# Feed-forward operands stored in four spaced quarters and read four columns at a time, last columns first

## The chip, the cores and the metric

The kernel runs on one core of one Trainium2 chip. The metric is device time in microseconds; the median of three runs of the kernel before is 530.65 us (530.53 to 530.72). The core works with five engines: TensorE (PE, matrix products; its weight loads are listed apart as PEld), VectorE (DVE), ScalarE (ACT), GpSimd (POOL) and SyncE (SP, which issues nearly all DMAs). Operands lie in the on-chip memory SBUF, in 128 partitions; TensorE writes its results to PSUM.

## The reference, cut to what matters

A gated recurrence over 768 steps, for 4 batches and 8 heads of width 48, gives a matrix x of 3072 tokens by 384 channels; a gated feed-forward layer follows.

```python
for t in range(S):                                  # S = 768, D = 48
    state = alpha[:, :, t, :, None] * state + k_t (x) v_t
    y[:, :, t] = q_t @ state
x = y.transpose(0, 2, 1, 3).reshape(3072, 384)
gate = 1 / (1 + exp(-(x @ w_gate)))                 # 384 x 1536
val = x @ w_val                                     # 384 x 1536
out = (gate * val) @ w_out                          # 1536 x 384
```

## The kernel before, in words

Tokens are taken in `NG` = 6 groups of `T` = 512. In each group the recurrence is worked out in chunks, by 4 units (pairs of heads); units 0 to 5 (function `unit`) use chunks of 128 tokens, units 6 to 23 (function `late`) chunks of 64. A unit ends in `finish`: ACT copies its output y from PSUM as a rounded high part (line 500, or line 489 in group 0), DVE subtracts that from y and stores the rest as a low part (lines 501 and 491), and, from group 1 on, SP moves both from the tile `yt` to the right partitions of `x` by DMA (line 508).

The feed-forward layer runs in 72 steps (function `step`), 12 blocks of 128 hidden channels in each of the 6 groups. All weights and the moving operands are split in such a high and a low part of type fp32r, and a product is taken as high by high, high by low and low by high (`PAIRS`). So a step has 9 matmuls for the gate and 9 for the value (line 297, three parts by three tiles of 128 input channels) and 9 for the output (line 741, three parts by three tiles of 128 output channels), 27 in all. Each loads its own 128x128 weights and streams 512 columns, one token each, of 4 bytes. Between them ACT takes the sigmoid (line 728), DVE multiplies (line 730), ACT rounds the product to `hh` (line 732) and DVE stores the rest in `hl` (line 733).

What is moved is read in order of its address: `xin(g)[:, i, b, :]` and `h[a][:, 0:T]` are 512 consecutive words of a partition. Tiles stand in SBUF one behind the other. The tile `between`, 40 words of which one is used, stands between `sg` and `hh`. By the sizes of the tiles, `x0`, `x1`, `hh`, `hl` and all weight tiles of the program before start at the same address modulo 512 bytes.

The order of the work on each engine is set when the program is built: `Plan` simulates the engines with estimated times, the table `MOVES` shifts single pieces, and the result is issued as it stands. Before the first product 60 places for bf16 matmuls on the identity matrix (line 705, `warm`) are planned, which nothing reads; those that come ahead of the first feed-forward product are issued.

Of the kernel before, what the change touches and what calls it, by code (L numbers as in the profile page):

```python
# [8 lines left out]
F32 = mybir.dt.float32  # L9
F32R = mybir.dt.float32r  # L10
# [6 lines left out]
ALU = mybir.AluOpType  # L17

P = 128
B, H, S, D = 4, 8, 768, 48  # L20
DM, DF = 384, 1536
# [16 lines left out]
    tuple(((2 * p + j) * D, p - 1, R * j, D) for p in range(1, NP) for j in range(2))  # L38
EARLY = 6
TURNED = 4  # L40


WIDTH = EH + 3 * T + 1
# [216 lines left out]
def vec(n):  # L260
    return 0.07 + n / 960


def act(n):
    return 0.13 + n / 1200
# [35 lines left out]
def chunked(ctx, tc, rows, vc, vh, weights_in, out, const, ident, flags, weights, within):  # L301
# [8 lines left out]
    def slot(tag, size):  # L310
        slots[tag] = [const.tile([P, size], F32, name=f"first_{tag}", tag=tag), 0]
        held[tag] = []

    for f in range(6, NF):
        slot(f"w{f}", 2 * WF)
    slot("x1", NK * 2 * T)

    def borrow(tag, *shape):
        t, at = slots[tag]
# [33 lines left out]
    tops = [(f"top{i}", sb.tile([P, WF // 2], U32, name=f"top{i}")) for i in range(3)]  # L353
    r_top = Ring(tops)
    r_kn = ring("kn", 1, CH, P, early=[borrow("w6", CH, P) for _ in range(2)])
    r_yt = ring("yt", 1, 2, T, dtype=F32R)
    r_A = ring("A", 2, 2, T, early=[borrow("x1", 2, T) for _ in range(2)])
    (pickn, pick), (sparen, spare) = borrow("w7", NK, P), borrow("w7", 2, T)
    pick, spare = pick.bitcast(F32R), spare.bitcast(F32R)
# [7 lines left out]
    tiny = sb.tile([P, EH], F32, name="tiny")  # L367
    starts = sb.tile([P, NG * NP, EH], F32, name="starts")
    sts = [sb.tile([P, EH + 1, D], F32, name=f"st{p}") for p in range(NP)]
    r_x = [const.tile([P, NK, 2, T], F32R, name="x0", tag="x0")]  # L370
    r_sg = ring("sg", 1, T)
    between = sb.tile([P, 40], F32, name="between")
    r_hh, r_hl = ring("hh", 2, T, dtype=F32R), ring("hl", 2, T, dtype=F32R)
    r_at = ring("at", 3, 512, pool=ps)
    r_pg, r_pv, r_po = ring("pg", 1, 512, pool=ps), ring("pv", 1, 512, pool=ps), ring("po", NM, 512, pool=ps)
    r_bank = Ring([*r_at.tiles, *r_po.tiles, *r_pg.tiles])
# [5 lines left out]
    nc.vector.memset(d1g[C][:, 0:T:C], 1.0)  # L382
    nc.vector.memset(d1f, 0.0)
    nc.vector.memset(tiny, 1e-30)
    nc.gpsimd.memset(mask[C], 1.0)
    nc.gpsimd.affine_select(out=mask[C], in_=mask[C], pattern=[[1, C]], compare_op=ALU.is_ge, fill=0.0, base=0, channel_multiplier=-1)

# [55 lines left out]

    def xin(g):
        if g % 2 == len(r_x):
            r_x.append(const.tile([P, NK, 2, T], F32R, name="x1", tag="x1"))
        return r_x[g % 2]

    def decays(u, size, t, inn, tin):
# [34 lines left out]
    def finish(g, p, t, pyn, py):  # L484

        x_n = f"x{g % 2}"
        if g == 0 and p:
            x, hi, lo = xin(0)[:, p - 1], (x_n, p - 1, "hi"), (x_n, p - 1, "lo")
            plan.add("scalar", act(T), t["y"], lambda: nc.scalar.copy(out=x[:, 0], in_=py[:, 0:T]), [pyn], [hi])
            plan.add("vector", vec(T), t["y"], lambda: nc.vector.tensor_tensor(  # L490
                out=x[:, 1], in0=py[:, 0:T], in1=x[:, 0], op=ALU.subtract), [pyn, hi], [lo])
            xparts.setdefault(0, []).extend([hi, lo])
            return
        if g == 0:
            plan.add("scalar", act(T), t["y"], lambda: nc.scalar.copy(out=spare[:, 0], in_=py[:, 0:T]), [pyn], [(sparen, "s")])
            plan.add("vector", vec(T), t["y"], lambda: nc.vector.tensor_tensor(
                out=spare[:, 1], in0=py[:, 0:T], in1=spare[:, 0], op=ALU.subtract), [pyn, (sparen, "s")], [(sparen, "k")])
            return
        ytn, yt = r_yt.next()
        plan.add("scalar", act(T), t["y"], lambda: nc.scalar.copy(out=yt[:, 0], in_=py[:, 0:T]), [pyn], [(ytn, 0)])  # L500
        plan.add("vector", vec(T), t["y"], lambda: nc.vector.tensor_tensor(
            out=yt[:, 1], in0=py[:, 0:T], in1=yt[:, 0], op=ALU.subtract), [pyn, (ytn, 0)], [(ytn, 1)])
        for ch, k, row, m in PLACES:
            j, src = divmod(ch, D)
            if j // 2 != p:
                continue
            src += R * (j % 2)
            plan.add("sync", (ISSUE, 0.3 + 0.6 * m * T * 8 / RATE), t["y"], lambda row=row, m=m, k=k, src=src: nc.sync.dma_start(
                out=xin(g)[row:row + m, k].bitcast(F32), in_=yt[src:src + m].bitcast(F32)), [(ytn, 0), (ytn, 1)],
                [(x_n, k, ch), *(before("x1") if g == 1 else [])])  # L510
            xparts.setdefault(g, []).append((x_n, k, ch))
# [200 lines left out]
    def step(s):  # L712
        g, f = divmod(s, NF)
        got = {}
        for nm, r, dt in (("g", r_pg, 0.0), ("v", r_pv, 0.33)):
            pn, pt = (r_three if g else r).next()
            got[nm] = (pn, pt)
            def ahead(nm=nm, pt=pt, tiles=None):
                if nm == "v":
                    opened.append(s)  # L720
                products(nc, pt[:, 0:T], lambda a, i: weights.part(nm, a, f)[:, i], lambda b, i: xin(g)[:, i, b, :], tiles)

            for tiles in ([range(NK - 1), range(NK - 1, NK)] if s < 2 else [range(NK)]):
                plan.add("tensor", (MM * 3 * len(tiles), 1.0), s + dt, lambda ahead=ahead, tiles=tiles: ahead(tiles=tiles),
                    [*weight(nm, f), *(x for x in xparts[g] if x[1] in tiles)], [pn])
        soon = s > NF + 2
        (sgn, sg), (hhn, hh), (hln, hl) = r_sg.next(), r_hh.next(), r_hl.next()
        plan.add("scalar", act(T), None, lambda: nc.scalar.activation(out=sg, in_=got["g"][1][:, 0:T], func=AF.Sigmoid), [got["g"][0]], [sgn], soon=soon)  # L728
        pvn, pv = got["v"][0], got["v"][1][:, 0:T]
        plan.add("vector", vec(T), None, lambda: nc.vector.tensor_tensor(out=pv, in0=pv, in1=sg, op=ALU.mult), [sgn], [pvn], soon=soon)  # L730
        last = s == NG * NF - 1
        plan.add("scalar", act(T), None, lambda: nc.scalar.copy(out=hh, in_=pv), [pvn], [hhn], soon=soon)  # L732
        plan.add("vector", vec(T), None, lambda: nc.vector.tensor_tensor(out=hl, in0=pv, in1=hh, op=ALU.subtract), [pvn, hhn], [hln], soon=soon)
        h = (hh, hl)
        if f == 0:
            pso[:] = [r_po.next() for _ in range(NM)]

        def back(m, some):
            for i in some:
                a, b = PAIRS[i]  # L740
                nc.tensor.matmul(out=pso_now[m][1][:, 0:T], lhsT=weights.part("o", b, f)[:, m * P:(m + 1) * P], rhs=h[a][:, 0:T],  # L741
                                 start=(f == 0 and i == 0), stop=(f == NF - 1 and i == 2))

        pso_now = list(pso)
        for some, hs in (((0, 1), [hhn]), ((2,), [hln])):
            for m in range(NM):
                plan.add("tensor", (MM * len(some), 1.0), s + 1 + 0.66 + (0.1 * m + 0.01 * some[0] - 0.5 if last else 0.01 * m + 0.1 * some[0]), lambda m=m, some=some: back(m, some),
                         [*hs, *weight("o", f)], [pso_now[m][0]])
        if f == NF - 1:
            for m in range(NM):  # L750
                (pn, pt), (on, to) = pso[m], ob[m]
                over = [(on, "u"), (on, "l")] if g == 0 else []
                halves = 2 if (m == NM - 1 if last else g in (3, 4)) else 1
                n = T // halves
                for half in range(halves):
                    cs, queue = slice(half * n, (half + 1) * n), "scalar" if last and m % 2 == 0 and half == halves - 1 else "sync"
                    if m % 2:
                        plan.add("vector", vec(n), s + 1.9, lambda pt=pt, to=to, cs=cs: nc.vector.tensor_copy(out=to[:, cs], in_=pt[:, cs]), [pn], [("ob", m, half), *over])
                    else:
                        plan.add("scalar", act(n), s + 1.9, lambda pt=pt, to=to, cs=cs: nc.scalar.copy(out=to[:, cs], in_=pt[:, cs]), [pn], [("ob", m, half), *over])  # L760
                    plan.add(queue, (ISSUE, n / T), s + 1.9, lambda to=to, m=m, cs=cs, queue=queue: getattr(nc, queue).dma_start(
                        out=out[m * P:(m + 1) * P, g * T + cs.start:g * T + cs.stop], in_=to[:, cs]), [("ob", m, half)])
# [60 lines left out]
def general(tc, rows, decay, values, out, weights):  # L823
# [3 lines left out]
    with ExitStack() as ctx:  # L827
# [32 lines left out]
        with tc.For_i(0, NG, 1) as g:  # L860
# [7 lines left out]
            for f in range(NF):  # L868
                pg, pv = (ps.tile([P, T], F32, name=f"gp{nm}") for nm in "gv")
                for nm, pt in (("g", pg), ("v", pv)):  # L870
                    products(nc, pt, lambda a, i: weights.part(nm, a, f)[:, i], lambda c, i: x[:, c, i])
                sg, hf, h = sb.tile([P, T], F32, name="gsg"), sb.tile([P, T], F32, name="ghf"), sb.tile([P, 2, T], F32R, name="gh")
                nc.scalar.activation(out=sg, in_=pg, func=AF.Sigmoid)
                nc.vector.tensor_tensor(out=hf, in0=pv, in1=sg, op=ALU.mult)
# [1 line left out]
                nc.vector.tensor_tensor(out=h[:, 1], in0=hf, in1=h[:, 0], op=ALU.subtract)  # L876
                for m in range(NM):
                    for n, (a, c) in enumerate(PAIRS):
                        nc.tensor.matmul(out=po[m], lhsT=weights.part("o", c, f)[:, m * P:(m + 1) * P], rhs=h[:, a],
                                         start=(f == 0 and n == 0), stop=(f == NF - 1 and n == 2))  # L880
            o = sb.tile([P, NM, T], F32, name="go")
            for m in range(NM):
# [58 lines left out]
```

## Time and profile before

| | |
|---|---|
| median of 3 runs | 530.65 us |
| profiled execution, first to last instruction (its span) | 528.8 us |
| between the span and the median of the runs | 1.85 us |
| PE busy | 519.7 us, 98% of the span |
| DVE busy | 398.7 us, 75% |
| ACT busy | 163.4 us, 31% |
| POOL busy | 88.5 us, 17% |
| granted TensorE clock | 0.999 of full speed |

The profile is of one execution. A matmul's duration there runs from its start to the modelled end of its results, and consecutive matmuls overlap; so what a chain of matmuls costs is read from the distance of their starts, not from the sum of durations. A group of n merged instructions in a timeline lasts n - 1 distances and one duration. DVE's share is uneven: over 95% from 30 to 90 us, 15% to 30% after 440 us, when the recurrence is done.

### The profile page before, as it was taken

To read this page: it belongs to the slowest core of one execution; us is meant where nothing else is said; L and a number is where in the kernel's file an instruction comes from. 1 tells how busy PE (TensorE), PEld (TensorE's weight loads), DVE (VectorE), ACT (ScalarE), POOL (GpSimd) and SP (SyncE) were. 2 spreads that over 40 slices of the span, in tenths; PEclk is the share of its full clock that TensorE was granted. 3 is DMA by queue.
4 is the path that set the end of the run, shared out by engine and by line. 5 is a ranking of instruction groups with operands and counts; after the bars stand their busy time and mean duration, and the time that the engine had idled before them with its cause. 6 is when DMAs were issued, how large, how long until landed. Compare 5 with 4: busy or idle time off the path is not lost.

```text
span 528.8 us, 10387 instructions
## 1 busy us (share of the span) xinstructions
PE 519.7 (98%) x4114; PEld 422.4 (80%) x4114; DVE 398.7 (75%) x866; ACT 163.4 (31%) x304; POOL 88.5 (17%) x127
## 2 busy tenths in 40 slices
PE   7999999999999999999999999999999999999996
PEld 3777888888888887888888888887888888888884
DVE  8999999888989999969888969889878532222221
ACT  2566666624112222222222321222322212311211
POOL 4532131103121122111121301211401100000000
PEclk9999999999999999999999999999999999999999
DMA  8757696830623333331423412403412011100001
GB/s 317 293 163 241 218 279 189 222 93 20 179 78 91 105 106 116 81 91 31 121 73 88 131 42 90 113 11 120 151 30 67 2 30 31 60 1 0 2 0 64
DMA packets 23093, 54.70 MB, mean 103 GB/s; under 512 B 3712, under 2 KB 10880, under 8 KB 23040
## 3 DMA queue, kind: packets, MB, share of 16 engines
q1 hardware_dynamic: 22752, 53.60, 33.8%
q8 instruction: 34, 0.56, 0.4%
q10 hardware_dynamic: 288, 0.39, 0.2%
q14 instruction: 19, 0.16, 0.1%
HBM read 41.39 MB, written 4.72 MB: 87 GB/s over the span
## 4 chain that ended last, share of the span: by engine, by line
PE 94%; DVE 4%; issue 0%; POOL 0%; ACT 0%; DVEq 0%
PE po L741 29%; PE pv L297 20%; PE pg L297 20%; PE at L297 16%; PE at L648 2%; PE pg L691 1%; PE at L655 1%; PE pv L691 1%; PE at L691 1%; DVE F L460 1%; DVE G L456 1%; PE at L476 1%; PE at L539 0%; PE pg L591 0%; PE pg L597 0%; DVE st L568 0%
## 5 line engine op out<-in xcount | busy, mean ns | idle before, releaser
L741 PE MATMUL po<-hh,w 128*128 128x512 f32 x432 | 116.1, 395 | 0.0
L297 PE MATMUL pv<-x,w 128*128 128x512 f32 x468 | 115.2, 390 | 0.0
L297 PE MATMUL pg<-x,w 128*128 128x512 f32 x459 | 112.9, 390 | 0.0
L297 PEld LDWEIGHTS pv<-x,w 128*128 128x128 f32 x468 | 87.6, 188 | 18.4
L297 PEld LDWEIGHTS pg<-x,w 128*128 128x128 f32 x459 | 85.9, 188 | 18.0 <-ACT w L428 0.2
L741 PEld LDWEIGHTS po<-hh,w 128*128 128x128 f32 x432 | 79.6, 188 | 17.0
L297 PE MATMUL at<-x,w 128*128 128x512 f32 x369 | 90.7, 390 | 0.1
L297 PEld LDWEIGHTS at<-x,w 128*128 128x128 f32 x369 | 69.1, 188 | 14.9 <-issue 0.5
L639 DVE STREAM_TRANSPOSE kn<-in 32x128 f32<-32x128 f32 x224 | 67.8, 303 | 5.0 <-PE at L655 1.2
L741 PE MATMUL po<-hl,w 128*128 128x512 f32 x216 | 64.4, 391 | 0.0
L679 POOL TENSOR_TENSOR vs<-st,dec 64x384 f32<-64x384 f32 x36 | 30.6, 850 | 162.3 <-DVE st L674 161.1
L464 POOL TENSOR_TENSOR in<-in,G 128x512 f32<-128x512 f32 x21 | 28.2, 1342 | 145.0 <-DVE G L456 46.9
L741 PEld LDWEIGHTS po<-hl,w 128*128 128x128 f32 x216 | 40.5, 188 | 8.7
L674 DVE SCALAR_TENSOR_TENSOR st<-st,dec,at 128x48 f32<-128x48 f32 x144 | 38.1, 264 | 7.7 <-PE at L655 1.9
L730 DVE TENSOR_TENSOR pv<-pv,sg 128x512 f32<-128x512 f32 x31 | 21.3, 687 | 29.7 <-PE pv L297 29.6
L730 DVE TENSOR_TENSOR at<-at,sg 128x512 f32<-128x512 f32 x21 | 14.4, 687 | 31.3 <-PE at L297 31.1
L732 ACT CAST hh<-pv 128x512 fp32r<-128x512 f32 x31 | 18.2, 586 | 55.1 <-DVE pv L730 55.1
L728 ACT ACTIVATE sg<-pg 128x512 f32<-128x512 f32 x31 | 18.5, 598 | 53.7 <-PE pg L297 53.7
L730 DVE TENSOR_TENSOR pg<-pg,sg 128x512 f32<-128x512 f32 x20 | 13.7, 687 | 27.1 <-PE pg L297 27.1
L661 DVE TENSOR_TENSOR A<-at,mask 64x256 f32<-64x256 f32 x72 | 30.4, 422 | 1.3
L728 ACT ACTIVATE sg<-pv 128x512 f32<-128x512 f32 x21 | 12.6, 598 | 50.1 <-PE pv L297 50.1
L460 DVE TENSOR_TENSOR_SCAN F<-in,d1f 128x512 f32<-128x512 f32 x22 | 27.6, 1257 | 0.3
(162 smaller groups left out, 508.1 us busy)
## 6 DMA issues: line engine op xcount, KB each, us to landing
in<-in_rows_dram SPq DMA_DIRECT2D x18, 516.5 KB, 3.9
raw<-in_w_dram SPq DMA_DIRECT2D x12, 575.8 KB, 4.7
x<-yt SPq DMA_DIRECT2D x30, 192.0 KB, 3.4
first_w<-in_w_dram SPq DMA_DIRECT2D x10, 575.8 KB, 4.9
A<-in_rows_dram SPq DMA_DIRECT2D x36, 128.0 KB, 3.9
v<-in_vc_dram SPq DMA_DIRECT2D x22, 192.0 KB, 5.0
vs<-in_vh_dram SPq DMA_DIRECT2D x36, 96.0 KB, 3.5
out_dram<-raw SPq DMA_DIRECT2D x10, 256.0 KB, 2.2
```

Source lines behind the costliest of these rows:

```text
L297: nc.tensor.matmul(out=dst, lhsT=lhs(a, i), rhs=rhs(b, i), start=(n == 0 and i == 0), stop=(n == len(todo) - 1 and i == NK - 1))
L460: plan.add("vector", scan(n), after(t["G"], 0.01), lambda: nc.vector.tensor_tensor_scan(out=F, data0=az[:, 0:n], data1=d1f, initial=0.0, o ...
L464: plan.add(e, vec(n) if e == "vector" else pool_(n), t["kt"], lambda: getattr(nc, e).tensor_tensor(out=kT, in0=kT, in1=G, op=ALU.mult), [g ...
L639: nc.vector.transpose(out=kn[32 * b:32 * b + 32, :, 32 * a:32 * a + 32], in_=blocks[32 * a:32 * a + 32, b])
L661: plan.add("vector", 0.42, t["mask"], lambda pa=pa, j=j, i=i: nc.vector.tensor_tensor(out=A[other[j], j].rearrange("p (c i t) -> p i c t", ...
L674: nc.vector.scalar_tensor_tensor(out=st[:, c + 1, :], in0=st[:, c, :], scalar=dec[:, c:c + 1], in1=pas[c % 2][1][:, T // 2 + c // 2 * D:T ...
L679: plan.add("gpsimd", pool_(EH * D), t["sd"], lambda j=j: nc.gpsimd.tensor_tensor(out=vs[own[j], j], in0=st[own[j], 0:EH], in1=dec[own[j]]. ...
L691: nc.tensor.matmul(out=py[R * j:R * j + D, cs], lhsT=vs[r, j, c, :], rhs=A[r, j, cs], start=True, stop=True)
L728: plan.add("scalar", act(T), None, lambda: nc.scalar.activation(out=sg, in_=got["g"][1][:, 0:T], func=AF.Sigmoid), [got["g"][0]], [sgn], s ...
L730: plan.add("vector", vec(T), None, lambda: nc.vector.tensor_tensor(out=pv, in0=pv, in1=sg, op=ALU.mult), [sgn], [pvn], soon=soon)
L732: plan.add("scalar", act(T), None, lambda: nc.scalar.copy(out=hh, in_=pv), [pvn], [hhn], soon=soon)
L741: nc.tensor.matmul(out=pso_now[m][1][:, 0:T], lhsT=weights.part("o", b, f)[:, m * P:(m + 1) * P], rhs=h[a][:, 0:T], start=(f == 0 and i == ...
```

## The change

Each tile of moving operands (`x0`, `x1`, `hh`, `hl`, and `yt`, from which x is filled) becomes 576 words long instead of 512 for each part: four quarters of 128 tokens, with 16 unused words behind each. So quarters start 576 bytes apart. The feed-forward matmuls read four words of the first quarter, four of the second, of the third, of the fourth, then the four words ahead of those in each, beginning with the last four of each quarter. The 512 columns reach PSUM in that order; h is stored in quarters of that order and read in turns again, and the array that comes back is put in the order of tokens by a transposed view.

The pieces of four words are 16 bytes and start at multiples of 16 bytes. The unused tiles `ahead` (40 words) and `behind` (24 words) and a longer `between` (76 words) place the moving tiles: all of `x0`, `x1`, `hh` and `hl` start at 192 modulo 256 bytes, all weight tiles at 32. The scratch space that is kept for DMA descriptors is halved, to make room.

```diff
+QUARTERS, BETWEEN, PIECE = 4, 16, 4
+LONG = T + QUARTERS * BETWEEN
+
+def quarters(t):
+    return t.rearrange("p (q t) -> p q t", q=QUARTERS)
+
+def stored(t):
+    return quarters(t)[:, :, 0:T // QUARTERS]
+
+def in_turns(t):
+    n = T // QUARTERS // PIECE
+    return t.rearrange("p (q m e) -> p m q e", q=QUARTERS, e=PIECE)[:, 0:n][:, ::-1]
...
-    slot("x1", NK * 2 * T)
+    const.tile([P, 40], F32, name="ahead", tag="ahead")
+    slot("x1", NK * 2 * LONG)
...
-    r_yt = ring("yt", 1, 2, T, dtype=F32R)
+    r_yt = ring("yt", 1, 2, LONG, dtype=F32R)
...
-    r_x = [const.tile([P, NK, 2, T], F32R, name="x0", tag="x0")]
+    r_x = [const.tile([P, NK, 2, LONG], F32R, name="x0", tag="x0")]
+    const.tile([P, 24], F32, name="behind", tag="behind")
     r_sg = ring("sg", 1, T)
-    between = sb.tile([P, 40], F32, name="between")
-    r_hh, r_hl = ring("hh", 2, T, dtype=F32R), ring("hl", 2, T, dtype=F32R)
+    between = sb.tile([P, 76], F32, name="between")
+    r_hh, r_hl = ring("hh", 2, LONG, dtype=F32R), ring("hl", 2, LONG, dtype=F32R)
...
+    for j in range(2):
+        nc.gpsimd.memset(quarters(r_yt.tiles[0][1][:, j])[:, :, T // QUARTERS:].bitcast(F32), 0.0)
     nc.gpsimd.memset(mask[C], 1.0)
...
-        plan.add("scalar", act(T), t["y"], lambda: nc.scalar.copy(out=yt[:, 0], in_=py[:, 0:T]), [pyn], [(ytn, 0)])
+        plan.add("scalar", act(T), t["y"], lambda: nc.scalar.copy(out=stored(yt[:, 0]), in_=quarters(py[:, 0:T])), [pyn], [(ytn, 0)])
...
-            out=yt[:, 1], in0=py[:, 0:T], in1=yt[:, 0], op=ALU.subtract), [pyn, (ytn, 0)], [(ytn, 1)])
+            out=stored(yt[:, 1]), in0=quarters(py[:, 0:T]), in1=stored(yt[:, 0]), op=ALU.subtract), [pyn, (ytn, 0)], [(ytn, 1)])
...
-                products(nc, pt[:, 0:T], lambda a, i: weights.part(nm, a, f)[:, i], lambda b, i: xin(g)[:, i, b, :], tiles)
+                products(nc, pt[:, 0:T], lambda a, i: weights.part(nm, a, f)[:, i], lambda b, i: in_turns(xin(g)[:, i, b, :]), tiles)
...
-        plan.add("scalar", act(T), None, lambda: nc.scalar.copy(out=hh, in_=pv), [pvn], [hhn], soon=soon)
-        plan.add("vector", vec(T), None, lambda: nc.vector.tensor_tensor(out=hl, in0=pv, in1=hh, op=ALU.subtract), [pvn, hhn], [hln], soon=soon)
+        plan.add("scalar", act(T), None, lambda: nc.scalar.copy(out=stored(hh), in_=quarters(pv)), [pvn], [hhn], soon=soon)
+        plan.add("vector", vec(T), None, lambda: nc.vector.tensor_tensor(out=stored(hl), in0=quarters(pv), in1=stored(hh), op=ALU.subtract), [pvn, hhn], [hln], soon=soon)
...
-                nc.tensor.matmul(out=pso_now[m][1][:, 0:T], lhsT=weights.part("o", b, f)[:, m * P:(m + 1) * P], rhs=h[a][:, 0:T],
+                nc.tensor.matmul(out=pso_now[m][1][:, 0:T], lhsT=weights.part("o", b, f)[:, m * P:(m + 1) * P], rhs=in_turns(h[a]),
...
-    nc = _bacc.Bacc("TRN2", target_bir_lowering=False, num_devices=1, dynamic_dma_scratch_size=8192)
+    nc = _bacc.Bacc("TRN2", target_bir_lowering=False, num_devices=1, dynamic_dma_scratch_size=4096)
...
-    return _np.ascontiguousarray(r.results[0]["out_0_dram"].T)
+    n = T // QUARTERS // PIECE // QUARTERS
+    y = r.results[0]["out_0_dram"].reshape(DM, NG, n, QUARTERS, QUARTERS, PIECE)[:, :, :, ::-1, ::-1]
+    return _np.ascontiguousarray(y.transpose(1, 3, 4, 2, 5, 0).reshape(B * S, DM))
```

Lines 489 and 491 change as lines 500 and 501 do. `Plan` and `MOVES` are not touched: PE, DVE, ACT and SP carry the same instructions in the same order in both programs, with other shapes (128x4x128 for 128x512) where a tile is stored in quarters. POOL gets two instructions more, the memsets of the unused words of `yt`, which stand between the memset and the affine select of the identity matrix.

## Rows read from the trace of the kernel before

**Rows 1.** The page, busy time: us, share of the span, instructions.

```profile
PE 519.7 (98%) x4114; PEld 422.4 (80%) x4114; DVE 398.7 (75%) x866; ACT 163.4 (31%) x304; POOL 88.5 (17%) x127
```

**Rows 2.** Waits of PE, whole span, first and last of six: us in total, times, longest.

```profile
PE pv L705 <- POOL ident masks.py:199: 1.6, 1, 1.6
...
PE po L539 <- POOL first_w L527: 0.2, 1, 0.2
```

**Rows 3.** The page, costliest groups: busy us, mean ns of one, idle before.

```profile
L741 PE MATMUL po<-hh,w 128*128 128x512 f32 x432 | 116.1, 395 | 0.0
L297 PE MATMUL pv<-x,w 128*128 128x512 f32 x468 | 115.2, 390 | 0.0
L297 PE MATMUL pg<-x,w 128*128 128x512 f32 x459 | 112.9, 390 | 0.0
L297 PEld LDWEIGHTS pv<-x,w 128*128 128x128 f32 x468 | 87.6, 188 | 18.4
L297 PE MATMUL at<-x,w 128*128 128x512 f32 x369 | 90.7, 390 | 0.1
L741 PE MATMUL po<-hl,w 128*128 128x512 f32 x216 | 64.4, 391 | 0.0
```

**Rows 4.** Timeline of PE near the end: start us, us.

```profile
515.30 2.20 PE L297 MATMUL pv<-x,w 128*128 128x512 f32 x9
517.34 2.20 PE L297 MATMUL at<-x,w 128*128 128x512 f32 x9
519.38 1.52 PE L741 MATMUL po<-hh,w 128*128 128x512 f32 x6
```

**Rows 5.** Timeline of PE, 10.3 to 11.6 us.

```profile
10.78 0.81 PE L705 MATMUL pv<-ident 128*128 128x512 bf16 x3
```

**Rows 6.** Groups on PE, 10.80 to 11.55 us.

```profile
L705 PE MATMUL pv<-ident 128*128 128x512 bf16 x3 | 0.8, 379 | 0.0
```

**Rows 7.** Line 297 on PE: duration in ns, least, median, most.

```profile
L297 PE MATMUL pg<-x,w x459: 388/389/501, 29.4 to 513.0; 128*128 128x512 f32 x153
```

**Rows 8.** Groups on PE, 200.95 to 202.05 us, behind a pause of the feed-forward matmuls.

```profile
L297 PE MATMUL pg<-x,w 128*128 128x512 f32 x6 | 1.7, 411 | 0.0
```

**Rows 9.** Windows, all engines: length, busy us and instructions of PE, PEld, DVE, ACT, POOL; clock, DMA.

```profile
30.00:90.00 60.00, 60.00 (x512) 49.09 (x511) 58.23 (x100) 39.26 (x68) 15.51 (x20) 1.00 0.73 229
90.00:150.00 60.00, 60.00 (x527) 49.48 (x527) 52.43 (x106) 21.94 (x39) 9.13 (x13) 1.00 0.45 121
150.00:211.80 61.80, 61.80 (x530) 50.65 (x520) 57.53 (x138) 15.49 (x30) 14.92 (x21) 1.00 0.36 106
211.80:440.00 228.20, 228.07 (x1916) 187.34 (x1911) 181.35 (x436) 56.13 (x107) 33.00 (x45) 1.00 0.27 74
```

**Rows 10.** Windows, line 297 on PE alone: length, busy us and matmuls.

```profile
30.00:90.00 60.00, 34.95 (x145) 1.00 0.73 229
150.00:211.80 61.80, 38.64 (x162) 1.00 0.36 106
```

**Rows 11.** Windows, line 741 on PE alone.

```profile
30.00:90.00 60.00, 16.78 (x63) 1.00 0.73 229
150.00:211.80 61.80, 20.94 (x82) 1.00 0.36 106
```

**Rows 12.** Waits of DVE, 30 to 90 us, the only one.

```profile
DVE pv L730 <- PE pv L297: 0.8, 2, 0.6
```

**Rows 13.** Waits of DVE, 150 to 211.8 us, first and last of four.

```profile
DVE pg L730 <- PE pg L297: 0.7, 1, 0.7
...
DVE st L674 <- PE at L655: 0.2, 1, 0.2
```

**Rows 14.** Groups on DVE by shape, 30 to 212 us: line 552 works on 4 blocks of 128.

```profile
L730 DVE TENSOR_TENSOR pv<-pv,sg 128x512 f32<-128x512 f32 x16 | 11.0, 688 | 2.6 <-PE pv L297 2.6
L552 DVE TENSOR_TENSOR A<-at,mask 128x512 f32<-128x512 f32 x4 | 2.6, 682 | 0.0
```

**Rows 15.** Timeline of POOL, 0 to 9 us.

```profile
8.31 1.56 POOL L464 TENSOR_TENSOR in<-in,G 128x512 f32<-128x512 f32 x1 [5.39 <-DVE G L456]
```

More of the change, by code (lines that the diff above doesn't have):

```diff
@@ L445, in xin @@
         if g % 2 == len(r_x):
-            r_x.append(const.tile([P, NK, 2, T], F32R, name="x1", tag="x1"))
+            r_x.append(const.tile([P, NK, 2, LONG], F32R, name="x1", tag="x1"))
         return r_x[g % 2]
@@ L488, in finish @@
             x, hi, lo = xin(0)[:, p - 1], (x_n, p - 1, "hi"), (x_n, p - 1, "lo")
-            plan.add("scalar", act(T), t["y"], lambda: nc.scalar.copy(out=x[:, 0], in_=py[:, 0:T]), [pyn], [hi])
+            plan.add("scalar", act(T), t["y"], lambda: nc.scalar.copy(out=stored(x[:, 0]), in_=quarters(py[:, 0:T])), [pyn], [hi])
             plan.add("vector", vec(T), t["y"], lambda: nc.vector.tensor_tensor(
-                out=x[:, 1], in0=py[:, 0:T], in1=x[:, 0], op=ALU.subtract), [pyn, hi], [lo])
+                out=stored(x[:, 1]), in0=quarters(py[:, 0:T]), in1=stored(x[:, 0]), op=ALU.subtract), [pyn, hi], [lo])
             xparts.setdefault(0, []).extend([hi, lo])
@@ L870, in general @@
                 for nm, pt in (("g", pg), ("v", pv)):
-                    products(nc, pt, lambda a, i: weights.part(nm, a, f)[:, i], lambda c, i: x[:, c, i])
+                    products(nc, pt, lambda a, i: weights.part(nm, a, f)[:, i], lambda c, i: in_turns(x[:, c, i]))
                 sg, hf, h = sb.tile([P, T], F32, name="gsg"), sb.tile([P, T], F32, name="ghf"), sb.tile([P, 2, T], F32R, name="gh")
@@ L878, in general @@
                     for n, (a, c) in enumerate(PAIRS):
-                        nc.tensor.matmul(out=po[m], lhsT=weights.part("o", c, f)[:, m * P:(m + 1) * P], rhs=h[:, a],
+                        nc.tensor.matmul(out=po[m], lhsT=weights.part("o", c, f)[:, m * P:(m + 1) * P], rhs=in_turns(h[:, a]),
                                          start=(f == 0 and n == 0), stop=(f == NF - 1 and n == 2))
```

## The prediction

> **What bounds the kernel now.** I read the busy times first, then what PE waits for, then its costliest groups, then its timeline, and last what DVE does in the same stretches. PE is busy 98% of the span [rows 1]. Busy is not the same as at its peak, so the waits come next: PE waited for another engine six times in the whole span, 1.6 us at most, and all six are on lines that prepare the identity matrix or belong to the first six units, at the start [rows 2]. So from the first feed-forward step on nothing but PE's own stream of matmuls sets the pace. What fills that stream are the feed-forward matmuls: 432 + 216 + 468 + 459 + 369 = 1944 of them [rows 3], which is 72 steps of 27.
>
> What one of them costs is the distance of starts. Near the end, where nothing else runs on PE, nine matmuls of line 297 begin at 515.30, the next nine at 517.34, those of line 741 at 519.38 [rows 4]: 2.04 us for nine, 226.7 ns each. 1944 x 226.7 ns = 440.7 us, 83% of the span of 528.8. [...] The bf16 matmuls on the identity have 512 columns too, and a weight load each. Three of them last 0.81 us [rows 5] at 0.379 each [rows 6], so their starts lie (0.81 - 0.379)/2 = 0.2155 us apart. The feed-forward matmul is 11.2 ns slower than that, and its duration, 389 ns at the median [rows 7], is longer by 10. 1944 x 11.2 ns = 21.8 us is the sum that the change can play for on PE.
>
> **Is this excess fixed?** If it were part of any fp32r matmul, no order of columns would move it. Two rows say that it is rather a stall of the stream. Where feed-forward matmuls set in again behind other work, six of them have a mean of 411 ns [rows 8]; the first is the 501 that includes its own weight load [rows 7], which leaves (6 x 411 - 501)/5 = 393 for the other five: same shape, same operands, but 4 ns longer than the settled 389. A fixed cost would not differ with the place in the chain. And the stream that does without it is the one with half the bytes in a column and with 128 columns that come back four times. So I take the 11.2 ns for stalls in reading 2048 bytes per partition in order at full rate, and that order is exactly what changes.
>
> [...]
>
> **The change part by part.**
>
> *Reading in turns.* Instructions, weight loads and columns are the same in number and order; what changes is the address of each column. [...] The nearest row of a stream that does not stall is the bf16 one, 215.5 ns, saving 21.8 us. [...] I take the bf16 row, 215.5, since it differs from the stalling one in bytes and addresses alone.
>
> *DVE.* With PE faster, DVE is late next. In 30 to 90 us it is busy 58.23 of 60 us [rows 9], and waits for PE 0.8 us [rows 12]; the other 0.97 us are steps between its instructions, so it needs 59.2 us. PE has 145 + 63 = 208 feed-forward matmuls there [rows 10, 11] and would need 60 - 208 x 0.0112 = 57.7. DVE holds back 1.5 us. In 150 to 211.8 us DVE is busy 57.53, waits 1.7 in four places (0.7 to 0.2) [rows 9, 13] and so needs 60.1; PE would need 61.8 - 244 x 0.0112 = 59.1: another 1.0 us. In 90 to 150 it has 52.43 of 60, behind 211.8 it has 181.35 of 228.2 [rows 9], and holds nothing back. Together 2.5 us; 0 if DVE's queue shifts work into the free stretches, and about as much again if waits come one by one.
>
> *Storing in quarters.* ACT's and DVE's writes of x, yt, hh and hl get four blocks of 128 for 512 in a row. DVE already does that form at line 552: 682 ns against 688 in a row [rows 14]. Nothing. ACT is 31% busy [rows 1] and could hide a difference of the same size.
>
> *More bytes for x.* The DMAs from yt move 576 words for each 512, an eighth more. They fill x for the next group, steps ahead of its first product; PE waits for none of them now [rows 2]. Nothing, and some tenths of a us if one comes late.
>
> *Two memsets on POOL*, ahead of the identity's affine select, may delay PE's first wait of 1.6 us by some tenths. What they delay are bf16 matmuls that nothing reads; POOL itself is idle 5.39 us ahead of its first work on data [rows 15]. Nothing.
>
> The sum: 528.8 - 21.8 + 2.5 = 509.5 for the span. The median of the runs lies 1.85 us above the profiled span, which nothing here touches: 511.4, and I say **512**.
>
> **The rivals.**
>
> *Half of it stays.* A weight load takes 188 ns [rows 3] of the 226.7, so a good part of each stream is read beside one. If the stalls come from the two reads meeting, turns may only thin them out. For it: the settled pace differs from the pace behind a pause, so something's phase matters. With half the excess, 5.6 x 1944 = 10.9 us go; DVE then holds back 0.4 in the first stretch (60 - 1.16 = 58.8 against 59.2) and nothing in the second. 530.65 - 10.9 + 0.4 = 520. [...]
>
> [...]
>
> *Slower.* Turns lose the settled pace. The addresses no longer run on from word to word, and each jump, or a start that lies otherwise to the weights, costs what the unsettled stream shows, 4 ns more [rows 7, 8]: 1944 x 4 = 7.8 us, 538.4. It decides as soon as the new stream is over 226.7 ns, since PE has no slack behind the start. Against it: a stream with jumps in these rows keeps the best pace of all, though with three jumps, not 127. If jumps cost more than that, the way up is long: 0.1 ns for each is 24.7 us.
>
> [...]
>
> **How the numbers follow.** 45% for the forecast (508 to 514, by DVE's share), 27% for the half (514 to 528), 11% for no change, 17% for slower. A measurement of this kernel can tell 0.2%, 1.1 us, from no change. So faster 0.72, same 0.11, slower 0.17. The range goes from 506, the forecast with nothing held back and part of what lies between 215.5 and 213.3, to 532, which takes in the first three cases; what it leaves out is most of the slower one.
>
> **What would show it.** Right: the duration of the feed-forward matmuls falls from 389 to about 378, nine of them start 1.94 us apart, and PE waits for DVE for some us between 30 and 212. Half: 383 or so and 1.99. No change: 389. Slower: over 389, with 2.04 passed. If durations fall and the time does not, look at DVE's waits and at PE's, which must then have grown from nothing. I am wrong if the settled distance does not move, whatever the reason given here.

## The result, and the profile after

The changed kernel takes 518.25 us (median of 4 runs, 517.93 to 518.71) against 530.68 us before; the ratio is 0.9768, with a 95% interval of 0.9754 to 0.9782. The profiled span went from 528.8 to 516.6 us, 12.2 us less. Line numbers after are 20 to 24 higher: the products of line 297 stand at line 317, those of line 741 at line 765.

The page of the changed kernel, busy time and costliest groups (columns as in [rows 1, 3]):

```profile
PE 506.4 (98%) x4114; PEld 422.1 (82%) x4114; DVE 397.4 (77%) x866; ACT 164.0 (32%) x304; POOL 88.6 (17%) x129
...
L765 PE MATMUL po<-hh,w 128*128 128x512 f32 x432 | 112.8, 387 | 0.0
L317 PE MATMUL pv<-x,w 128*128 128x512 f32 x468 | 111.9, 382 | 0.0
...
L317 PEld LDWEIGHTS pv<-x,w 128*128 128x128 f32 x468 | 87.6, 188 | 15.3
...
L317 PE MATMUL at<-x,w 128*128 128x512 f32 x369 | 88.2, 382 | 0.8 <-DMA x<-yt 0.8
L765 PE MATMUL po<-hl,w 128*128 128x512 f32 x216 | 62.9, 383 | 0.0
```

Every feed-forward group is 8 ns shorter than in [rows 3]; a weight load still takes 188 ns, and the busy times of the other engines have moved by 1.3 us at most. The timeline of PE near the end (start, length), which answers to [rows 4]:

```profile
503.02 2.14 PE L317 MATMUL pv<-x,w 128*128 128x512 f32 x9
505.00 2.14 PE L317 MATMUL at<-x,w 128*128 128x512 f32 x9
506.99 1.48 PE L765 MATMUL po<-hh,w 128*128 128x512 f32 x6
```

Nine matmuls now take (506.99 - 503.02)/2 = 1.985 us, 220.6 ns each for 226.7. Over the whole trace I took the starts of consecutive feed-forward matmuls, leaving out pauses (distances of 300 ns and more): their mean distance fell from 227.1 to 220.2 ns, so 1944 x 6.9 = 13.4 us. The span gained 1.2 us less. Part of that are two waits that the list of before does not have. Waits of PE (us in total, times, longest), as in [rows 2], the first of all and these two:

```profile
PE pv L729 <- POOL ident masks.py:199: 1.6, 1, 1.6
...
PE at L317 <- DMA x<-yt: 0.8, 1, 0.8
...
PE at L672 <- POOL starts L489: 0.3, 1, 0.3
```

Only the wait for POOL is wholly new: the same matmul waited for the DMA before too, 0.13 us, which is too short for that list. All idle time of PE went from 4.0 to 4.8 us. So 0.8 us show as waits, and 0.4 us remain without a name. The wait for the DMA lies in the timeline of PE at the start of a group's products (the pause ends with the DMA that fills x). First the same place before, then after:

```profile
366.14 2.04 PE L297 MATMUL at<-x,w 128*128 128x512 f32 x6
```

```profile
357.47 0.72 PE L317 MATMUL at<-x,w 128*128 128x512 f32 x2
358.98 1.34 PE L317 MATMUL at<-x,w 128*128 128x512 f32 x5 [0.79 <-DMA x<-yt]
```

The chain that ended last, followed back from this wait (start, length), runs through DVE, which writes `yt`, and the DMA that SP issues behind it (SPq is its queue):

```profile
352.94 0.70 DVE yt L525
353.66 0.54 SPq L532
354.24 4.60 DMA x<-yt
```

DVE in the stretch in which I had it late (windows, columns of [rows 9], and its waits, as in [rows 12]):

```profile
30.00:90.00 60.00, 60.00 (x520) 50.37 (x519) 58.86 (x103) 40.89 (x68) 15.52 (x20) 1.00 0.76 232
```

```profile
DVE pv L754 <- PE pv L317: 0.2, 1, 0.2
DVE w L454 <- ACT w L452: 0.2, 1, 0.2
```

DVE is at 98%, its wait for PE has shrunk from 0.8 to 0.2 us, and PE still never stops there.

### The profile page after: what moved, and what is told of

It reads as the page before. It is cut to its first block, busy times and chain, and to the rows that moved or that the text cites. A ratio compares the mean times of both kernels' runs of the same rounds, so it can differ in the third digit from the quotient of the medians.

```text
span 516.6 us, 10389 instructions
## 1 busy us (share of the span) xinstructions
PE 506.4 (98%) x4114; PEld 422.1 (82%) x4114; DVE 397.4 (77%) x866; ACT 164.0 (32%) x304; POOL 88.6 (17%) x129
## 4 chain that ended last, share of the span: by engine, by line
PE 88%; DVE 7%; DMA 2%; issue 1%; POOL 1%; ACT 0%; SPq 0%; DVEq 0%
PE po L765 26%; PE pv L317 19%; PE pg L317 18%; PE at L317 15%; PE at L672 2%; PE pg L715 1%; PE at L679 1%; DMA A<-in_rows_dram 1%; PE pv L715 1%; DVE G L480 1%; DMA x<-yt 1%; DVE kn L663 1%; PE at L715 1%; DVE F L484 1%; PE at L500 1%
## 5 line engine op out<-in xcount | busy, mean ns | idle before, releaser
L765 PE MATMUL po<-hh,w 128*128 128x512 f32 x432 | 112.8, 387 | 0.0
L317 PE MATMUL pv<-x,w 128*128 128x512 f32 x468 | 111.9, 382 | 0.0
L317 PE MATMUL pg<-x,w 128*128 128x512 f32 x459 | 109.7, 382 | 0.0
L317 PE MATMUL at<-x,w 128*128 128x512 f32 x369 | 88.2, 382 | 0.8 <-DMA x<-yt 0.8
L765 PE MATMUL po<-hl,w 128*128 128x512 f32 x216 | 62.9, 383 | 0.0
L650 DVE TENSOR_TENSOR A<-A,F 64x512 f32<-64x512 f32 x36 | 25.8, 717 | 3.4 <-DMA A<-in_rows_dram 2.6
L756 ACT CAST hh<-at 128x512 fp32r<-128x512 f32 x21 | 12.3, 586 | 50.7 <-DVE at L754 50.7
```

The lines of the kernel that those rows point to most:

```text
L317: nc.tensor.matmul(out=dst, lhsT=lhs(a, i), rhs=rhs(b, i), start=(n == 0 and i == 0), stop=(n == len(todo) - 1 and i == NK - 1))
L650: plan.add("vector", vec(T), t["q"], lambda j=j: nc.vector.tensor_tensor(out=A[own[j], j], in0=A[own[j], j], in1=F[own[j]], op=ALU.mult), ...
```

## The experiments

Two theories stood at the beginning. **O**: the stream stalls on reading consecutive words, by itself; turns spare that. **M**, later sharpened to **R**: the stream's reads meet those of the weight load beside it, so what counts is how the two lie to one another. The expectations of e7 and e8 also name **A**: what counts is where the moving tile starts, whatever the weights do. "Place" below is the start of the moving tile less that of the weights, modulo 256 bytes: 0 before, 160 in the change. (In the change the parts of x start 2304 bytes apart, so they lie at two places modulo 512: there the means of the nine matmuls of a product lie between 220.0 and 220.7 ns. That the place repeats every 256 bytes no other run shows.) "Distance" is the mean between starts worked out as above, and each time stands against the kernel before on the same chip.

| run | order | place | distance ns | us | before us |
|---|---|---|---|---|---|
| before | in order | 0 | 227.1 | 530.7 | |
| after | turns, from the end | 160 | 220.2 | 518.3 | 530.7 |
| e1_place | in order | 160 | 234.3 | 544.1 | 530.8 |
| e2_forward | turns, from the start | 160 | 228.2 | 532.7 | 530.8 |
| e3_phase0 | turns, from the end | 0 | 226.9 | 529.9 | 530.8 |
| e4_half | in order, half the weight columns | 0 | 229.7 | 535.6 | 530.8 |
| e5_in_order_end | in order, from the end | 160 | 233.3 | 542.3 | 530.6 |
| e6_no_space | turns, quarters 512 bytes apart | 160 | 270.6 | 614.3 | 530.6 |
| e7_both | in order, all tiles shifted | 0 | 227.1 | 531.1 | 530.6 |
| e8_scan | turns, from the end | six others | 225.4 | 527.4 | 530.6 |
| e9_order_scan | in order | six others | 231.7 | 539.3 | 531.0 |
| e10_fine | turns, from the end | 144, 176, 160 | 221.9 | 521.1 | 531.0 |
| e11_piece8 | turns of 8 columns | 160 | 230.0 | 536.2 | 531.0 |
| e12_weights_moved | turns, from the end | 96 and 160 | 222.3 | 522.3 | 530.4 |

The times of e1 to e3 are medians of 4 to 10 runs, those of e4 to e12 single runs. In all but the last line the time follows the distance alone: 1944 times the difference to 227.1 gives the difference in time within 1 us (e6: 1944 x 43.5 = 84.6 us against 83.7). In e12 it would give 9.4 us less and 8.1 were measured; PE's idle time comes to 5.6 us there against 4.0 before, 2.0 of them for a DMA to v at the start that no other run shows.

**e1_place.** Placing alone, still in order.

```diff
+    const.tile([P, 40], F32, name="ahead", tag="ahead")
     slot("x1", NK * 2 * T)
...
+    const.tile([P, 88], F32, name="behind", tag="behind")
...
-    between = sb.tile([P, 40], F32, name="between")
+    between = sb.tile([P, 80], F32, name="between")
```

> The kernel before with the moving tiles placed as in the changed one (192 modulo 256 bytes, weights at 32), still read in order. Theory O (the stream stalls on reading consecutive words at full rate, and turns spare half of it): placing does nothing, settled distance 227 ns, time 530.7. Theory M (the stream's reads meet those of the weight load beside it, so that their relative place decides): the distance moves; if placing is the whole gain, 220 ns and 518; a bad place could also give more than 227.

13 us slower (ratio 1.0253, 1.0236 to 1.027). Timeline of PE, e1_place:

```profile
524.17 2.27 PE L297 MATMUL pg<-x,w 128*128 128x512 f32 x9
526.28 1.57 PE L743 MATMUL po<-hh,w 128*128 128x512 f32 x6
```

Nine take 2.11 us where [rows 4] have 2.04. Same instructions, same order of words, another address: theory O, by which the place does nothing, is wrong. This does not say that order does nothing: see e9.

**e2_forward.** The quarters from their start.

```diff
-    return t.rearrange("p (q m e) -> p m q e", q=QUARTERS, e=PIECE)[:, 0:n][:, ::-1]
+    return t.rearrange("p (q m e) -> p m q e", q=QUARTERS, e=PIECE)[:, 0:n]
```

> The changed kernel read in turns from the start of the quarters instead of the end. Theory O: the direction does not matter, 220 ns and 518.2. Theory M: the weight load runs in one direction, so the direction counts: over 220 ns, at most the 227 of before, 519 to 531.

All of the gain and some more is gone (ratio 1.0037, 1.0023 to 1.0052), 1 ns and 2 us beyond what M had set: at this place the direction counts, 228.2 ns from the start against 220.2 from the end. That the weight load runs in one direction was an assumption of M's; no run shows it. Reading from the start was tried at no other place.

**e3_phase0.** Turns from the end, at place 0 (`ahead` left out, `behind` of 64 and `between` of 40 words).

> The changed kernel with the moving tiles at the same place modulo 256 bytes as the weights (both 32). Theory O: nothing changes, 220 ns, 518.2. Theory M: another distance, 222 to 231 ns, 522 to 540.

Ratio 0.9983 (0.9974 to 0.9993): at place 0, turns and direction are worth 0.2%. M had the right side in all three.

**e4_half.** Half as much weight data beside the stream, in seven of the nine matmuls of a gate or value product; the kernel leaves out half of the hidden sums there. These matmuls also write 64 partitions of PSUM instead of 128, so two things change.

```diff
-        nc.tensor.matmul(out=dst, lhsT=lhs(a, i), rhs=rhs(b, i), start=(n == 0 and i == 0),
+        m = P if n == 0 or n == len(todo) - 1 else P // 2
+        nc.tensor.matmul(out=dst[0:m], lhsT=lhs(a, i)[:, 0:m], rhs=rhs(b, i), start=(n == 0 and i == 0),
```

> The kernel before, with 64 of 128 weight columns in 7 of the 9 gate and value matmuls of each product (half of the hidden sums are left out there). Theory M: with half as much weight data read beside it the stream stalls about half as much, so those matmuls lie 219 to 222 ns apart instead of 227. Theory O: 227 as before, whatever the weights' width. The time follows: 1296 x 7/9 = 1008 matmuls, 5 to 8 us less with M, none with O.

Neither theory had this: the distances leave 227, as O does not allow, but upwards, as M does not. The weight loads did shrink, from 188 to 134 ns, but two half-loaded matmuls lie 230.0 ns apart, where M had 219 to 222. The median of line 298 hardly differs from [rows 7] (line on PE, least, median, most):

```profile
L298 PE MATMUL pv<-x,w x468: 387/390/505, 31.0 to 522.1; 128*64 128x512 f32 x102, 128*128 128x512 f32 x54
```

The spread does: where nearly all durations before are 389 ns, nine in ten here lie between 387 and 398, and distances of 224, 227, 230, 234 and 236 ns are all frequent. So the loss is not a price for each byte of weights. That it depends on when the load falls into the stream would fit, but no run changes that moment alone. It would fit too that the stream needs some matmuls to settle behind a pause: before, typical distances there are 231, 236, 228, 232, 231 and then 227 ns.

**e5_in_order_end.** In order, backwards, at place 160 (e1_place with `::-1` on both moving operands).

> Read in order but from the last word to the first, tiles of 512 words placed at 192 modulo 256 (weights at 32): the direction and the place of the change without turns. If turns are needed: at least the 227 ns of before, 530 or more. If direction and place are enough: 220 ns and 518.

233.3 ns: direction and place without turns are a loss of 12 us against before.

**e6_no_space.** `BETWEEN` = 0, other pads set for the same places.

> The changed kernel with no words between the quarters, which then start 512 bytes apart, so all four at one place modulo 256 bytes. If the spread of the quarters over 256 bytes is what spares stalls: the distance goes back to 227 to 235 ns, 531 to 545. If only the order of pieces counts: 220 ns and 518.

The slowest of all, 84 us over before and far beyond the 545 that I had set as the end. Timeline of PE, e6_no_space:

```profile
590.23 2.60 PE L317 MATMUL at<-x,w 128*128 128x512 f32 x9
592.66 2.62 PE L317 MATMUL pg<-x,w 128*128 128x512 f32 x9
595.12 1.80 PE L763 MATMUL po<-hh,w 128*128 128x512 f32 x6
```

270 to 273 ns each. With pieces that follow one another 512 bytes apart a matmul takes 50 ns more than with 576 bytes, 270.6 against 220.2. The number of jumps is the same in both, so this cost hangs on the address that they land on. Whether the weight load has a part in these 50 ns, or the stream alone, no run shows.

**e7_both.** One pad of 40 words ahead of all weights and moving tiles of the kernel before, which separates R from A.

> The kernel before with weights and moving tiles both shifted by 160 bytes, to 192 modulo 256. Theory R (what counts is how the stream lies to the weights): 227 ns and 530.7 as before. Theory A (what counts is where the moving tiles start by themselves): the 234 ns and 544 of the run in which the moving tiles alone were put there.

Line 297 on PE in e7_both (least, median, most), to be held against [rows 7]:

```profile
L297 PE MATMUL pg<-x,w x459: 387/389/501, 29.4 to 513.2; 128*128 128x512 f32 x153
```

227.1 ns and 531.1 us: a shift of both by 160 bytes changes nothing (227.1 ns before), that of one of them (e1) costs 13 us. A is wrong, R had it.

**e8_scan.** The changed kernel, six tiles at six places, by pads between them.

> The changed kernel with its six moving tiles at six places behind the weights modulo 256 bytes: x0 192, x1 128, hh0 96, hh1 224, hl0 32, hl1 64 (160 in the change). Theory R: mean distances differ by tile, from 220 to 231 ns, and the time lies at 522 to 536. If 160 is only one of several good places, one or two tiles keep 220. Theory A: x0, hh1, hl1 and the others differ by their own start, not by the distance to the weights.

x0 (192) 226.2, x1 (128) 225.8, hh0 (96) 224.3, hh1 (224) 224.1, hl0 (32) 224.1, hl1 (64) 224.2 ns: all better than in order, none at 220. Since products of different tiles follow one another here, a tile's number may hold some effect of its neighbours, which no run tells apart.

**e9_order_scan.** The same in the kernel before.

> The kernel before, read in order, with its moving tiles at the six places behind the weights that were not seen yet: x1 32, x0 64, hh0 96, hh1 128, hl0 192, hl1 224 bytes (0 gave 227 ns, 160 gave 234). If a place alone could have given the gain, one tile shows 220 to 224 ns. If reading in order is bound to meet the weight load often, all lie at 227 to 236 ns, and the time at 531 to 545.

x1 (32) 233.1, x0 (64) 229.6, hh0 (96) 233.1, hh1 (128) 232.1, hl0 (192) 230.9, hl1 (224) 232.2 ns. The kernel before already had the best of the eight places tried for reading in order, so a place alone was not to be had.

Held against e8, this says more. Distances in order and in turns, by place (0 and 160 from before, e3, e1 and after; the other six from one tile each, not the same in both runs, and perhaps with an effect of its neighbours):

| place | 0 | 32 | 64 | 96 | 128 | 160 | 192 | 224 |
|---|---|---|---|---|---|---|---|---|
| in order, ns | 227.1 | 233.1 | 229.6 | 233.1 | 232.1 | 234.3 | 230.9 | 232.2 |
| turns from the end, ns | 226.9 | 224.1 | 224.2 | 224.3 | 225.8 | 220.2 | 226.2 | 224.1 |

Turns are ahead at every place, by 0.2 ns at place 0 and by 14.1 at 160. Place 0 is the best for order and the worst for turns, which is why neither half of the change, taken from the kernel before, shows what it is worth.

**e10_fine.** x1 and x0 shifted by 16 bytes, the length of one piece (a "line" in the expectations), to either side.

```diff
+    def moved(tag):
+        t = const.tile([P, NK * 2 * LONG + 8], F32R, name=tag, tag=tag)[:, 4:4 + NK * 2 * LONG]
+        return t.rearrange("p (k b t) -> p k b t", k=NK, b=2)
```

> The changed kernel with x1 at 144 and x0 at 176 bytes behind the weights, 16 to either side of the 160 of the change; hh and hl stay at 160. If 160 is one step of a broad best place: 220 to 222 ns for one of them, 518 to 521. If the steady pace hangs on the very line: 222 to 228 ns for both, 521 to 528. A faster pace than 220 on one side would show as less than 518.

x1 at 144: 220.3, as good as 160. x0 at 176: 224.3, half-way between two paces, 220 and 231 ns, which are equally frequent there (172 and 173 distances). So the steady 220 ns is kept at 144 and 160, and only part of the time at 176.

**e11_piece8.** `PIECE` = 8.

> The changed kernel with pieces of eight columns (32 bytes) instead of four, all else alike. If only the spread over the four quarters counts: 220 ns and 518. If a piece must be one line of 16 bytes, so that consecutive lines lie 64 bytes apart: half of the way back, 222 to 230 ns, 522 to 537.

Line 317 on PE in e11_piece8:

```profile
L317 PE MATMUL pg<-x,w x459: 389/392/502, 29.4 to 518.5; 128*128 128x512 f32 x153
```

230.0 ns, at the far end of the second case: two consecutive pieces of 16 bytes out of one quarter give back all of the gain and 3 ns more, though reading in order at this place (e1, e5) is slower still.

**e12_weights_moved.** All moving tiles stay; the weights of blocks 0 to 5 move by 64 bytes, and so do the scratch tiles of the recurrence, `yt` and `sg`, which serve all blocks alike.

```diff
-    const.tile([P, 24], F32, name="behind", tag="behind")
+    const.tile([P, 40], F32, name="behind", tag="behind")
...
-    between = sb.tile([P, 76], F32, name="between")
+    between = sb.tile([P, 60], F32, name="between")
```

> The changed kernel with every moving tile where it was and the weights of blocks 0 to 5 alone moved up by 64 bytes; those of blocks 6 to 11 stay. Theory R: only the products of blocks 0 to 5 leave the steady 220 ns, for 223 to 227 (96 bytes behind the weights now), blocks 6 to 11 keep 220; time 521 to 525. If the stream met something else than the weights (itself, the results, another engine), all blocks keep 220 ns and the time stays at 518.

Blocks 0 to 5: 224.1 ns, blocks 6 to 11: 220.5. Groups on PE in the last token group of this run, first in blocks 0 to 5, then in blocks 6 to 11 (mean ns of one):

```profile
L317 PE MATMUL pg<-x,w 128*128 128x512 f32 x27 | 6.5, 385 | 0.0
L317 PE MATMUL pv<-x,w 128*128 128x512 f32 x27 | 6.5, 385 | 0.0
```

```profile
L317 PE MATMUL pg<-x,w 128*128 128x512 f32 x18 | 4.3, 382 | 0.0
L317 PE MATMUL pv<-x,w 128*128 128x512 f32 x17 | 4.1, 382 | 0.0
```

Within one run, the same moving words in the same order cost 3.6 ns more where only the weights lie elsewhere. So what counts is how the moving words lie to the weights, as R has it; how a weight load holds up the stream no run shows. None of the runs beats the change; 160 is the best place that was tried.

## Why the prediction was right, and where it was not

*What bounds the kernel.* Right: PE's stream set the time, and the time follows the distance of its matmuls within 1 us in all kernels but e12.

*Is the excess fixed?* Right that it is not: the distance ranged from 220.2 to 234.3 ns with the same words read at other places or in another order, and e6 lies far above, at 270.6. But the step "So I take the 11.2 ns for stalls in reading 2048 bytes per partition in order at full rate, and that order is exactly what changes" failed. Where the moving tile lies to the weights changes the time too (e1, e7, e12), and it decides what order is worth: 0.2 ns at place 0 (e3), 14.1 at 160. The prediction put no price on the placing as a gain; a start that lies otherwise to the weights stands in it only among the reasons for slower. By its reasoning e2 and e3, with the same turns, would have come to 512 as well; they came to 532.7 and 529.9. That the time of the change lies inside the range is luck to that extent. The bf16 stream that I took as the case without stalls has other weights too, and so differed in more than "bytes and addresses alone". Their weight load in the kernel before, 10.80 to 11.55 us, takes 97 ns (second number), against 188 in [rows 3]:

```profile
L705 PEld LDWEIGHTS <-ident 128*128 128x128 bf16 x2 | 0.2, 97 | 0.1
```

*Reading in turns.* The term was mis-sized: 215.5 ns was taken, 220.2 measured, 13.4 us of 21.8. Why 215.5 is not reached, no run shows. The 213.3 ns that the low end of the range, 506, counts on in part are shown by no run either: the shortest distance of two matmuls with 512 columns is 215 ns after, between bf16 matmuls, and 220 between feed-forward matmuls. The main forecast, 508 to 514, did not come. The rival "half of it stays" named the weight load, on whose place to the stream the distance depends (227.1 ns in e7, 234.3 in e1; 224.1 and 220.5 in e12); that the two reads meet stays its assumption, which no run shows by itself. It put the time at 520 against 518.25, and its signs, 383 ns and 1.99 us for nine, are nearer to the measured 381 (median of line 317) and 1.985 than the 378 and 1.94 of the full gain.

*DVE.* 2.5 us were set for the full gain; by the same working the gain that came, 6.9 ns, would leave 60 - 208 x 0.0069 = 58.6 against 59.2, so 0.6 us in the first stretch and nothing in the second. PE did not wait in that stretch at all. The step that failed is the 59.2 us as DVE's fixed need: the 100 DVE instructions that start from 29.9 us on before, and the same ones after, were busy 58.6 and then 57.9 us, with idle times of 1.8 and then 1.1 us, so they kept up. What came late was a DMA to x, 0.8 us, which I had priced at "some tenths of a us if one comes late", and once POOL, 0.3 us. The transfer itself is hardly longer (4.54 us before, 4.60 after, with an eighth more bytes). By the chain above it is DVE that comes late: its instruction on `yt` starts 8.1 us earlier than before (361.03, now 352.94), while PE arrives 8.7 us earlier (366.14, now 357.47). So DVE does hold PE back, but behind 211.8 us, where the prediction had nothing. The same matmul waits 0.4 us in e7, at the pace of before, and not at all in the runs that are 8 us or more slower.

*The rest.* Storing in quarters cost nothing. Groups on DVE and ACT, before and after:

```profile
L733 DVE TENSOR_TENSOR hl<-pv,hh 128x512 fp32r<-128x512 f32 x31 | 21.3, 686 | 4.2 <-ACT hh L732 3.9
L732 ACT CAST hh<-pv 128x512 fp32r<-128x512 f32 x31 | 18.2, 586 | 55.1 <-DVE pv L730 55.1
```

```profile
L757 DVE TENSOR_TENSOR hl<-pv,hh 128x512 fp32r<-128x512 f32 x31 | 21.3, 686 | 4.2 <-ACT hh L756 3.9
L756 ACT CAST hh<-pv 128x512 fp32r<-128x512 f32 x31 | 18.2, 587 | 54.8 <-DVE pv L754 50.9 <-PE po L765 2.0 <-DVE st L698 1.9
```

The memsets on POOL are seen in its timeline, and PE's first wait stayed at 1.6 us, as the lines on its waits show:

```profile
0.96 0.24 POOL L408 MEMSET yt<- 128x64 f32 x2
```

*Slower.* Turns could have cost time, as e6 shows (614.3 against 518.3 us, 96 us between the two spacings). A price for each of the 127 jumps, as in "0.1 ns for each is 24.7 us", can't say when: the number of jumps is the same in both, and what differs is the address that they land on.

## What to carry to other kernels

Where fp32r matmuls start farther apart than bf16 matmuls with as many columns in the same trace (here 227.1 against the 215.5 ns of the three in [rows 5, 6]), the place of the moving words to the weights may have a part in it: with the order kept, it alone was worth 7.2 ns here (e1) and 3.6 (e12). Where both operands start modulo 256 bytes can be worked out from the sizes of the tiles, and a pad of some words shifts it. Order, spacing, direction and place work together: with one of them missing in all tiles the result lay between 3 us faster (e8, a single run) and 84 us slower than before, so such a change must be tried as a whole and its parts by taking one away. Read the distance from starts over the whole trace: there it gives the time of all but one variant within 1 us. Near the quiet end alone it can mislead: the last 300 distances give 220.4 ns for e10 and 232.9 for e9, and with them times some 3 us off.

## What the runs showed of the hardware that was not expected

The stream has a steady pace and others. In the kernel before, most distances are 226 or 227 ns (1710 of 1884), and after nearly all are 220 (1816 of 1885); where the place is not right, distances wander, over 228 to 238 ns in e1 and over 219 to 230 in e8. Pieces 512 bytes apart, read one after the other, cost 50 ns a matmul against pieces 576 bytes apart (e6, 270.6 against 220.2). Half as much weight data beside the stream (e4) made it slower, not faster: 229.7 ns against 227.1.

It stays open how the place of the weights acts on the stream, whether the 50 ns of e6 have the same cause, and why 220 and not the 215.5 ns of the bf16 matmuls: no run took the weight load away, since each matmul here loads its own.
